# The output products of a second MoE with both halves of each weight side by side as 512 moving columns

## The chip, the cores and the metric

The kernel runs on one core of one Trainium2 chip. The metric is the device time of one launch in microseconds (us), from the host's order to the end of the last store. Before the change it is 1485.99 us, the median of three runs (1485.76 to 1487.83).

Engines are named as in the profile: PE (TensorE: matmuls, and PEld its weight loads), DVE (VectorE), ACT (ScalarE), POOL, and SP (SyncE), whose queue here issues every DMA of the kernel. In a matmul the stationary operand ("weights" to PE) is loaded first, 128x128; the other operand moves through the array column by column, up to 512 columns, and the product is added up in a PSUM bank of 2 KB per partition, of which there are eight.

## The reference

An attention block writes 4352 tokens of 512 numbers (8 groups of 512 tokens and 32 states). They go through a first MoE (512 to 2048, squared ReLU, back to 512) and then a second one, whose back half is what is changed here:

```
xn  = x / sqrt(mean(x*x) + 1e-6) * rms_g
g   = xn @ w_gate          # 512 -> 1536
val = xn @ w_val
out = (g / (1 + exp(-g)) * val) @ w_out     # 1536 -> 512
```

## The kernel before

All matrix products keep nearly the precision of fp32: each operand is split in a high part `hi` (a cast, on ACT) and a low part `lo` (the rest, a subtraction on DVE; `split`, lines 121 to 123), and each product is three matmuls, hi·hi, hi·lo and lo·hi. The second MoE also multiplies 2x2 block matrices with seven products in place of eight (`PRODUCTS`): sums of the blocks are made before (`wq_sums`, `w2_sums`, `h_sums`), and `recombine` (lines 580 to 600) adds the seven products up after.

The second MoE's front half (`moe2_in`, line 718) runs over four pairs `s` of token groups, and twelve chunks `fc` of 128 of the 1536 hidden numbers, with line 126 to 128 matmuls of 512 moving columns. Its results are stored in DRAM as `hq_dr[s, m]`, six chunks `m` of seven 128x512 blocks each (four blocks of the matrix and three of their sums; `h_store`, lines 780 and 781). The 32-token states of all groups together are a block of 256 tokens, which stays in SBUF (`hs`).

The back half begins with that state block (`moe2_out_sb`): 72 matmuls of 512 columns with the plain weights, of which it needs tiles 0 and 1 of each `m` alone. Then come eight blocks of 256 tokens of each group of a pair (`moe2_out`). For each block and each `m` two loads bring the seven blocks back (`hb`, four of them, 512 KB, line 834; `hc`, three, 384 KB, line 835), ACT and DVE split them, and for each of the seven products `k` and each half `c` of 128 tokens three matmuls of 256 columns follow (line 859): the token block is stationary, the weights move. The seven products of a block fill seven PSUM banks for all six `m`; at the last `m` `recombine` empties them in `ox` and `oy`, which are stored with 512 KB each (line 877).

The weights of the back half, `w2`, are summed and split while the first MoE runs, kept in DRAM, and loaded into SBUF near the end of the front half (line 816; four tiles of 512 KB for each `m`: tiles 0 and 1 the hi and lo of the four plain blocks, tiles 2 and 3 the hi and lo of the sums).

What runs in which order is written out: every step is put at a position (`put(pos, step)`), in units of one step of the matmul loop, all are sorted, and each engine gets its instructions in that order. The offsets stand in the table `T` (`wq` is the load of the front half's weights, `hst` the stores of `hq_dr`, `w2l` the weights' loads, `hbl` and `hbs` the loads and the splits of the back half). SP's queue is strictly in that order as well: a store that waits for DVE holds up all the loads behind it. `u(...)` takes one of 54 slots of 4 KB per partition in SBUF.

Of the kernel before, what the change touches and what calls it, by code (L numbers as in the profile page):

```python
# [57 lines left out]
def attention_moe_kernel(  # L58
# [521 lines left out]
    def hi_of(t, n=None):  # L580
        hi = u([P, 2, 512], F32R, "hi")
        src = f(t) if n is None else f(t)[:, :n, :]
        nc.scalar.copy(hi if n is None else hi[:, :n, :], src)
        return hi

    def lo_of(t, hi):
        lo = u([P, 2, 512], F32R, "lo")
        nc.vector.tensor_tensor(lo, f(t), f(hi), op=ALU.subtract)
        return lo
# [147 lines left out]
            hg[s, fc] = y  # L737

    def moe2_in_sb(fc):
        cols = slice((fc % 2) * P, (fc % 2 + 1) * P)  # L740
# [12 lines left out]
        product(v, "s1", "b11", True)  # L753
        product(v, "a22", "t4", False)
        q, r = divmod(fc, 4)
        if r == 0:
            hs[q] = u([P, 4, 256], F32, "hs")
        t = u([P, 2, 512], F32, "rg")
        nc.scalar.activation(t[:, 0, :n], g, AF.Silu)
        nc.vector.tensor_tensor(hs[q][:, r, :], t[:, 0, :n], v, op=ALU.mult)  # L760

    def h_sums(s, m):

# [11 lines left out]
    def h_store(s, m):  # L775
# [28 lines left out]

    def w2_split(m, i):
        after(("w2s", m, i))
        t = w2s[m][i]
        hi = hi_of(t)
        lo = lo_of(t, hi)
        nc.sync.dma_start(w2_dr[m, 2 * i], f(hi))  # L810
        nc.sync.dma_start(w2_dr[m, 2 * i + 1], f(lo))

    def load_w2(m, i):
        after(("ldw2", m, i), ("w2s", m, i // 2))
        w2q[m, i] = u([P, 2, 512], F32R, "w2")
        nc.sync.dma_start(f(w2q[m, i]), w2_dr[m, i])  # L816

    B_AT = dict(b11=(0, 0), b21=(0, 2), b22=(0, 3), t1=(2, 0), t2=(2, 1), t3=(2, 2), t4=(2, 3))

    def w2_part(m, name):  # L820
        i, q = B_AT[name]
        return tuple(
            w2q[m, i + j].rearrange("p a (q m) -> p (a q) m", q=2)[:, q, :] for j in range(2)
        )


    hb = {}

    def load_hb(blk, m):
        s, ob = divmod(blk, 2)  # L830
        cols = slice(256 * ob, 256 * ob + 256)
        after(("ldhb", blk, m), ("hst", s, m))
# [3 lines left out]
        hb[blk, m] = t  # L836

    def split_hb(blk, m, i):
        t = hb[blk, m][i]
        n = 4 - i  # L840
        hi, lo = u([P, 4, 256], F32R, "hh"), u([P, 4, 256], F32R, "hl")
        split(t[:, :n, :], hi[:, :n, :], lo[:, :n, :])
        hb[blk, m][i] = (hi, lo)
# [3 lines left out]
    def moe2_out(blk, m, k):
        a, b = PRODUCTS[k]
        last = m == NF2 // 2 - 1
        if m == 0:  # L850
            acc2[blk, k] = any_bank("o2")
        ps = acc2[blk, k]
        i, q = divmod(A_ROW.index(a), 4)
        hi, lo = (t[:, q, :] for t in hb[blk, m][i])
        w_hi, w_lo = w2_part(m, b)
# [9 lines left out]
        if not last:  # L865
# [4 lines left out]
        pv = ps.rearrange("p (c d) -> p c d", c=2)  # L870
        recombine(k, pv, (ox[:, :, :256], ox[:, :, 256:]), (oy[:, :, :256], oy[:, :, 256:]))
        s, ob = divmod(blk, 2)
        for i, done in ((0, 5), (1, 6)):
            if k == done:
                b = 2 * s + i
                rows = out[b * NT : b * NT + S, :].rearrange("(p c) m -> p c m", c=4)
                nc.sync.dma_start(rows[:, 2 * ob : 2 * ob + 2, :], acc2[blk][i])

    def split_hs(q):
        hi, lo = u([P, 4, 256], F32R, "hh"), u([P, 4, 256], F32R, "hl")  # L880
        split(hs[q], hi, lo)
        hs[q] = (hi, lo)

    def moe2_out_sb(fc):
        if fc == 0:
            acc2[SB, 0], acc2[SB, 1] = any_bank("o2"), any_bank("o2")
        q, r = divmod(fc, 4)
        hi, lo = hs[q]
        w_hi, w_lo = w2q[fc // 2, 0][:, fc % 2, :], w2q[fc // 2, 1][:, fc % 2, :]
        for c in range(2):  # L890
            cols = slice(c * P, (c + 1) * P)
            mm3(acc2[SB, c], hi[:, r, cols], lo[:, r, cols], w_hi, w_lo, fc == 0, fc == NF2 - 1)
        if fc < NF2 - 1:
            return
        t = u([P, 2, 512], F32, "os")
        nc.scalar.copy(t[:, 0, :], acc2[SB, 0])
        nc.vector.tensor_copy(t[:, 1, :], acc2[SB, 1])
        for c in range(2):
            for q in range(4):
                r0 = (4 * c + q) * NT + S  # L900
                nc.sync.dma_start(out[r0 : r0 + NS, :], t[32 * q : 32 * q + 32, c, :])
# [101 lines left out]
    for fc in range(NF2):
        put(n2 + fc / 2, moe2_out_sb, fc)
    for q in range(NF2 // 4):
        put(n2 + 2 * q + T["hs"], split_hs, q)
    for blk in range(B):
        e = n2 + (blk + 1) * nout
        for m in range(nout):
            for k in range(7):  # L1010
                put(e + m + k / 7, moe2_out, blk, m, k)
            put(e + m + T["hbl"], load_hb, blk, m)
            put(e + m + T["hbs0"], split_hb, blk, m, 0)
            put(e + m + T["hbs1"], split_hb, blk, m, 1)
# [168 lines left out]
```

## Time and profile before

| what | value |
|---|---|
| median of three runs | 1485.99 us |
| the profiled execution, its own time | 1484.66 us |
| its span, first to last instruction | 1482.6 us |
| granted TensorE clock, mean | 0.990 |
| PE busy | 1447.2 us, 98% of the span |
| DVE, ACT busy | 76%, 53% |
| the state block of the back half, PE | 1216.4 to 1232.6 us |
| its eight blocks, PE | 1232.6 to 1477 us |

The span is about 2.1 us shorter than the execution's own time. PE's busy time counts a matmul until its modelled end, and these ends overlap the next matmul, so a matmul's cost is read from the distance of two starts in the timeline, not from its length. A row of waits names who ended an idle time; a row of the chain names what the end of the program rests on.

### The profile page before, as it was taken

What the parts mean: (1) busy time and instruction counts of PE and PEld (TensorE: products, weight loads), DVE (VectorE), ACT (ScalarE), POOL (GpSimd) and SP (SyncE); (2) the same over time, 40 slices, a digit from 0 to 9 for tenths busy, and PEclk for the clock granted to TensorE, in tenths of its full rate; (3) what the DMA queues carried; (4) which work ended last, traced back from release to release, by engine and by line L of the source; (5) the groups of instructions that cost most, each with busy time, mean ns of one, the idle gap of its engine ahead of it and who ended that gap; (6) DMA issues with size and microseconds to landing.
All of it is one profiled execution on the core that took longest, in us unless ns stands there. A gap on an engine that the chain in (4) does not pass through costs nothing. (4 is left out here: it accounts for less than half of the span.)

```text
span 1482.6 us, 20652 instructions
## 1 busy us (share of the span) xinstructions
PE 1447.2 (98%) x7706; PEld 1248.6 (84%) x7706; DVE 1125.2 (76%) x1654; ACT 783.0 (53%) x1186; POOL 0.7 (0%) x6
## 2 busy tenths in 40 slices
PE   4899999999999999999999999999999999999998
PEld 2688888888888888889987888888888888999998
DVE  7997878999998999874778878978965664565554
ACT  5988768888888888874522211312311123434331
POOL 0000000000000000000000000000000000000000
PEclk7999999999999999999999999999999999999999
DMA  8886443464555555452957897797786869567753
GB/s 321 291 282 226 149 163 121 163 235 166 226 176 219 178 220 180 170 208 72 355 213 279 324 347 282 284 354 279 264 315 221 292 238 339 182 218 242 241 188 107
DMA packets 138420, 345.82 MB, mean 233 GB/s; under 512 B 12112, under 2 KB 56144, under 8 KB 138320
## 3 DMA queue, kind: packets, MB, share of 16 engines
q1 hardware_dynamic: 138320, 344.51, 64.6%
q8 instruction: 60, 0.98, 0.3%
q14 instruction: 40, 0.33, 0.1%
HBM read 229.12 MB, written 115.34 MB: 232 GB/s over the span
## 5 line engine op out<-in xcount | busy, mean ns | idle before, releaser
L126 PE MATMUL p<-hi,wq 128*128 128x512 f32 x672 | 261.7, 389 | 2.0 <-DVE hx L594 2.0
L127 PE MATMUL p<-lo,wq 128*128 128x512 f32 x672 | 261.6, 389 | 0.0
L128 PE MATMUL p<-hi,wq 128*128 128x512 f32 x672 | 261.4, 389 | 0.0
L859 PE MATMUL o<-w,hh 128*128 128x256 f32 x1344 | 242.1, 283 | 0.8 <-ACT hh L122 0.8
L734 ACT ACTIVATE hx<-hx 128x1024 f32<-128x1024 f32 x48 | 50.9, 1061 | 332.9 <-DVE hx L594 332.9
L126 PE MATMUL o<-hl,wh 128*128 128x512 f32 (+1 forms) x576 | 218.8, 380 | 1.1 <-DVE x L518 0.8
L128 PE MATMUL o<-hl,wl 128*128 128x512 f32 (+1 forms) x576 | 217.6, 378 | 0.0
L127 PE MATMUL o<-hl,wh 128*128 128x512 f32 (+1 forms) x576 | 217.5, 378 | 0.0
L859 PEld LDWEIGHTS o<-w,hh 128*128 128x128 f32 x1344 | 209.6, 192 | 1.3 <-ACT hh L122 1.3
L859 PE MATMUL o<-w,hl 128*128 128x256 f32 x672 | 190.4, 283 | 0.8 <-DVE hl L123 0.8
L594 DVE TENSOR_TENSOR hx<-hx,p 128x512 f32<-128x512 f32 x192 | 128.9, 683 | 52.6 <-PE p L128 49.6
L126 PEld LDWEIGHTS p<-hi,wq 128*128 128x128 f32 x672 | 126.2, 188 | 28.2 <-DVE hx L594 2.4
L128 PEld LDWEIGHTS p<-hi,wq 128*128 128x128 f32 x672 | 126.2, 188 | 26.4
L127 PEld LDWEIGHTS p<-lo,wq 128*128 128x128 f32 x672 | 126.2, 188 | 25.5
L490 DVE TENSOR_TENSOR hl<-rg,hl 128x512 fp32r<-128x512 f32 (+1 forms) x144 | 94.6, 657 | 54.3 <-ACT hl L489 53.4
L859 PEld LDWEIGHTS o<-w,hl 128*128 128x128 f32 x672 | 129.0, 192 | 1.1 <-DVE hl L123 1.0
L126 PEld LDWEIGHTS o<-hl,wh 128*128 128x128 f32 x576 | 108.4, 188 | 22.8 <-DVE x L518 2.8
L128 PEld LDWEIGHTS o<-hl,wl 128*128 128x128 f32 x576 | 108.4, 188 | 20.3
L127 PEld LDWEIGHTS o<-hl,wh 128*128 128x128 f32 x576 | 108.4, 188 | 19.8
L126 PE MATMUL h<-at,ph 128*128 128x512 f32 x256 | 102.1, 399 | 5.0 <-ACT pst L260 5.0
L123 DVE TENSOR_TENSOR hl<-hb,hh 128x1024 fp32r<-128x1024 f32 x48 | 58.7, 1222 | 57.1 <-ACT hh L122 57.1
L122 ACT CAST hh<-hb 128x1024 fp32r<-128x1024 f32 x48 | 50.4, 1050 | 95.9 <-DMA hb<-hq_dr 94.6
(169 smaller groups left out, 2592.9 us busy)
## 6 DMA issues: line engine op xcount, KB each, us to landing
wq<-wq_dr SPq DMA_DIRECT2D x168, 512.0 KB, 7.2
hq_dr<-hy SPq DMA_DIRECT2D x48, 512.0 KB, 3.6
hb<-hq_dr SPq DMA_DIRECT2D x48, 512.0 KB, 8.5
hc<-hq_dr SPq DMA_DIRECT2D x48, 384.0 KB, 8.7
raw<-in_moe_w_out_dram SPq DMA_DIRECT2D x30, 512.0 KB, 6.6
p_dr<-pst SPq DMA_DIRECT2D x56, 256.0 KB, 5.5
praw<-p_dr SPq DMA_DIRECT2D x28, 512.0 KB, 5.3
wq_dr<-hi SPq DMA_DIRECT2D x24, 512.0 KB, 2.9
```

The costliest lines, as they stand in the source:

```text
L122: nc.scalar.copy(hi, src)
L123: nc.vector.tensor_tensor(lo, src, f(hi), op=ALU.subtract)
L126: nc.tensor.matmul(ps, lh, rh, start=start, stop=False)
L127: nc.tensor.matmul(ps, lh, rl, start=False, stop=False)
L128: nc.tensor.matmul(ps, ll, rh, start=False, stop=stop)
L490: nc.vector.tensor_tensor(t[:, 1, :n], rg[:, 1, :n], f(t[:, 0, :n]), op=ALU.subtract)
L594: add = lambda o, i, p: nc.vector.tensor_tensor(o, i, p, op=ALU.add)
L734: nc.scalar.activation(x, x, AF.Silu)
L859: mm = lambda l, r, start, stop: nc.tensor.matmul(o, l, r, start=start, stop=stop, skip_group_check=True)
```

## The change

The changed kernel keeps the number of products, and each product's three terms, but feeds PE in other pieces. The hi and the lo of a block of `w2` now lie side by side in 512 columns (`w2_split` writes them so, `load_w2` brings three full tiles and one half tile for each `m`). A product of 128 tokens is then one matmul of 512 columns (the tokens' hi against hi and lo of the weights) and one of 256 (the tokens' lo against the weights' hi, into the first half of the bank). The two halves of the bank are added at the very end, on DVE, in `os` (line 893), which is stored with 256 KB.

A bank now holds 128 tokens, not 256, so there are 17 blocks, the states as the first of them: they go through the seven products too, with `hs_sums` (four DVE operations of 128x128 for each `m`), and need all the tiles of `w2`. Within a block the six `m` are done in two halves of three, product by product. Loads are for a pair of blocks (256 tokens, as before), splits for each block of 128 (128x512 and 128x384). Several offsets of `T` differ.

```
-    wq0=-6.06, wq=-1.9, wq_gap=0.27,
+    wq0=-6.06, wq=-4.0, wq_gap=0.33,
...
+    def hs_sums(m):
...
+        nc.vector.tensor_tensor(a[4], a[1], a[3], op=ALU.add)
+        sub(5, 4, 0)
+        sub(1, 0, 1)
+        sub(6, 2, 5)
...
     def load_w2(m, i):
-        after(("ldw2", m, i), ("w2s", m, i // 2))
-        w2q[m, i] = u([P, 2, 512], F32R, "w2")
-        nc.sync.dma_start(f(w2q[m, i]), w2_dr[m, i])
-    B_AT = dict(b11=(0, 0), b21=(0, 2), b22=(0, 3), t1=(2, 0), t2=(2, 1), t3=(2, 2), t4=(2, 3))
+        after(("ldw2", m, i), ("w2s", m, i))
+        n = 1 if i == 3 else 2
+        w2q[m, i] = u([P, 2, 2, 256], F32R, "w2")
+        nc.sync.dma_start(f(w2q[m, i])[:, :n], w2_dr[m, i][:, :n])
+    B_AT = dict(b11=(0, 0), b21=(0, 1), t1=(1, 0), t2=(1, 1), t3=(2, 0), t4=(2, 1), b22=(3, 0))
...
-        for c in range(2):
-            o = ps[:, 256 * c : 256 * c + 256]
-            cols = slice(c * P, (c + 1) * P)
-            mm = lambda l, r, start, stop: nc.tensor.matmul(
+        for m in range(half * HALF, (half + 1) * HALF):
+            hi, lo = hq[blk, m]
+            w = w2_part(m, b)
+            mm = lambda o, l, r, start, stop: nc.tensor.matmul(
                 o, l, r, start=start, stop=stop, skip_group_check=True
             )
-            mm(hi[:, cols], w_hi, m == 0 and c == 0, False)
-            mm(hi[:, cols], w_lo, False, False)
-            mm(lo[:, cols], w_hi, False, last)
+            mm(ps, hi[:, i, :], w, m == 0, False)
+            mm(ps[:, :256], lo[:, i, :], w[:, :256], False, m == 2 * HALF - 1)
...
+                o = u([P, 2, 256], F32, "os")
+                nc.vector.tensor_tensor(o, t[:, :, :256], t[:, :, 256:], op=ALU.add)
...
+    for q, blk in enumerate([2 * B] + list(range(2 * B))):
+        e = n2 + q * nout
         for m in range(nout):
+            h, r = divmod(m, HALF)
+            if blk < 2 * B and blk % 2 == 0:
+                put(e + HALF * h + T["hbl"] + T["hbl_gap"] * r, load_hb, blk // 2, m)
+            put(e + HALF * h + T["hbs"] + T["hbs_gap"] * r, split_hb, blk, m)
```

How the order moves is shown at three places. In the rows a name carries the tile's numbers (`w2_dr5_3` is `m` 5, tile 3; `hq_dr0_1` pair 0, `m` 1; numbers behind a second underscore only count tiles), and an L is the line in the kernel concerned.

The first place is SP's queue at the passage from the front half to the back half. Before, behind the four stores of `hq_dr3_4`:

```order
L816 DMA w2_2150_11112<-w2_dr5_1_192 128x1024
L816 DMA w2_2153_11120<-w2_dr4_2_189 128x1024
L816 DMA w2_2154_11122<-w2_dr3_3_186 128x1024
L780 DMA hq_dr3_5_170<-hy_2116_10901 128x1024
L780 DMA hq_dr3_5_170<-hy_2133_11003 128x1024
L780 DMA hq_dr3_5_170<-sa_2151_11114 128x1024
L781 DMA hq_dr3_5_170<-sa_2152_11115 128x512
L816 DMA w2_2157_11150<-w2_dr5_2_193 128x1024
L816 DMA w2_2158_11152<-w2_dr4_3_190 128x1024
L834 DMA hb_2159_11160<-hq_dr0_0_147 128x4x256
L835 DMA hc_2160_11161<-hq_dr0_0_147 128x3x256
L816 DMA w2_2161_11170<-w2_dr5_3_194 128x1024
```

After, behind the same four stores and two full loads (`w2_dr4_2` and `w2_dr5_0`):

```order
L830 DMA w2_2163_11191<-w2_dr4_3_190 128x512
L830 DMA w2_2164_11193<-w2_dr5_1_192 128x1024
L830 DMA w2_2171_11217<-w2_dr5_2_193 128x1024
L849 DMA hb_2173_11226<-hq_dr0_0_147 128x4x256
L850 DMA hc_2174_11227<-hq_dr0_0_147 128x3x256
L793 DMA hq_dr3_5_170<-hy_2123_10953 128x1024
L793 DMA hq_dr3_5_170<-hy_2142_11062 128x1024
L793 DMA hq_dr3_5_170<-sa_2159_11181 128x1024
L794 DMA hq_dr3_5_170<-sa_2160_11182 128x512
L849 DMA hb_2175_11234<-hq_dr0_1_148 128x4x256
L850 DMA hc_2176_11235<-hq_dr0_1_148 128x3x256
L830 DMA w2_2177_11238<-w2_dr5_3_194 128x512
```

The last tile of the weights, `w2_dr5_3`, stands behind one more pair of `hb` and `hc` loads than before, and the state block now needs it; the loads of the first blocks, `hb` and `hc` of `hq_dr0_0`, moved ahead of the stores of `hq_dr3_5`.

The second place is a turn from one 256 tokens to the next. SP's queue before, with the stores of the first block of pair 0:

```order
L877 DMA out_0_dram<-ox_2216_11534 128x1024
L877 DMA out_0_dram<-oy_2217_11535 128x1024
L834 DMA hb_2225_11601<-hq_dr0_4_151 128x4x256
L835 DMA hc_2226_11602<-hq_dr0_4_151 128x3x256
L834 DMA hb_2237_11661<-hq_dr0_5_152 128x4x256
L835 DMA hc_2238_11662<-hq_dr0_5_152 128x3x256
L834 DMA hb_2243_11715<-hq_dr1_0_153 128x4x256
L835 DMA hc_2244_11716<-hq_dr1_0_153 128x3x256
L834 DMA hb_2249_11769<-hq_dr1_1_154 128x4x256
L835 DMA hc_2250_11770<-hq_dr1_1_154 128x3x256
L834 DMA hb_2255_11823<-hq_dr1_2_155 128x4x256
L835 DMA hc_2256_11824<-hq_dr1_2_155 128x3x256
```

After, from the stores of a block that is the first of its two:

```order
L903 DMA out_0_dram<-os_2335_12102 128x512
L903 DMA out_0_dram<-os_2336_12112 128x512
L849 DMA hb_2348_12168<-hq_dr1_0_153 128x4x256
L850 DMA hc_2349_12169<-hq_dr1_0_153 128x3x256
L849 DMA hb_2350_12172<-hq_dr1_1_154 128x4x256
L850 DMA hc_2351_12173<-hq_dr1_1_154 128x3x256
L849 DMA hb_2352_12176<-hq_dr1_2_155 128x4x256
L850 DMA hc_2353_12177<-hq_dr1_2_155 128x3x256
L849 DMA hb_2364_12250<-hq_dr1_3_156 128x4x256
L850 DMA hc_2365_12251<-hq_dr1_3_156 128x3x256
```

Before, the stores of a block are followed by loads for `m` 4 and 5 of the next block and for the first of the one after it. After, the stores of the first block of 128 tokens are followed by the loads of the next 256 tokens from `m` 0 on; all six `m` are behind these stores, and the next two stores are behind all of them.

DVE's order around these stores after the change, with the sums of the first block of two (`ox`, `oy`, `os`) and the splits for the second (`hl`):

```order
L595 TENSOR_TENSOR oy_2328_12046<-ox_2327_12045,o2_2318_11992 128x512
L124 TENSOR_TENSOR hl_2332_12069<-hb_2292_11862,hh_2331_12068 128x512
L124 TENSOR_TENSOR hl_2332_12069<-hc_2293_11863,hh_2331_12068 128x384
L595 TENSOR_TENSOR ox_2327_12045<-ox_2327_12045,o2_2321_12005 128x512
L595 TENSOR_TENSOR oy_2328_12046<-oy_2328_12046,o2_2321_12005 128x512
L124 TENSOR_TENSOR hl_2334_12083<-hb_2294_11866,hh_2333_12082 128x512
L124 TENSOR_TENSOR hl_2334_12083<-hc_2295_11867,hh_2333_12082 128x384
L595 TENSOR_TENSOR ox_2327_12045<-ox_2327_12045,o2_2324_12018 128x512
L595 TENSOR_TENSOR ox_2327_12045<-ox_2327_12045,o2_2325_12025 128x512
L893 TENSOR_TENSOR os_2335_12102<-ox_2327_12045 128x512
L595 TENSOR_TENSOR oy_2328_12046<-oy_2328_12046,o2_2326_12032 128x512
L893 TENSOR_TENSOR os_2336_12112<-oy_2328_12046 128x512
```

The stores of the two `os` stand at the end of the sums of a block, behind the splits of the next block's first three `m`.

The third place is SP's queue in the first pair of the front half. Before:

```order
L657 DMA wq_1480_7615<-wq_dr4_2_135 128x1024
L657 DMA wq_1484_7636<-wq_dr4_3_136 128x1024
L780 DMA hq_dr0_2_149<-hy_1435_7369 128x1024
L780 DMA hq_dr0_2_149<-hy_1450_7446 128x1024
L780 DMA hq_dr0_2_149<-sa_1467_7547 128x1024
L781 DMA hq_dr0_2_149<-sa_1468_7548 128x512
L657 DMA wq_1487_7660<-wq_dr4_6_139 128x1024
L657 DMA wq_1494_7685<-wq_dr5_0_140 128x1024
```

After:

```order
L658 DMA wq_1470_7559<-wq_dr4_6_139 128x1024
L658 DMA wq_1474_7571<-wq_dr5_0_140 128x1024
L560 DMA xn_dr8_102<-x2_1388_7139 128x2x256
L658 DMA wq_1477_7592<-wq_dr5_1_141 128x1024
L658 DMA wq_1482_7617<-wq_dr5_4_144 128x1024
L658 DMA wq_1485_7637<-wq_dr5_5_145 128x1024
L560 DMA xn_dr8_102<-x2_1387_7136 128x2x256
L658 DMA wq_1491_7668<-wq_dr5_2_142 128x1024
L658 DMA wq_1494_7687<-wq_dr5_3_143 128x1024
L793 DMA hq_dr0_2_149<-hy_1442_7407 128x1024
L793 DMA hq_dr0_2_149<-hy_1457_7484 128x1024
L793 DMA hq_dr0_2_149<-sa_1479_7603 128x1024
```

The load of `wq_dr4_6` stood behind the four stores of `hq_dr0_2`. After the change it stands nine rows ahead of the first of them, and six loads of `wq_dr5` stand ahead of them too.

## Rows read from the trace of the kernel before

**Rows 1.** Busy time of each engine over the span, the page's first part.

```profile
PE 1447.2 (98%) x7706; PEld 1248.6 (84%) x7706; DVE 1125.2 (76%) x1654; ACT 783.0 (53%) x1186; POOL 0.7 (0%) x6
```

**Rows 2.** Waits of PE from 600 us to the end: total, times, longest.

```profile
PE p L126 <- DVE hx L594: 2.0, 1, 2.0
PE o L859 <- ACT hh L122: 0.8, 1, 0.8
PE o L859 <- DVE hl L123: 0.8, 1, 0.8
```

**Rows 3.** Windows of the back half: busy (count) by engine, PEclk, DMA share, GB/s.

```profile
1216.40:1232.60 16.20, 16.20 (x74) 13.32 (x72) 5.19 (x7) 1.12 (x2) 0.00 (x0) 1.00 1.04 401
1232.60:1477.00 244.40, 242.81 (x2018) 242.08 (x2016) 133.79 (x152) 91.23 (x105) 0.00 (x0) 1.00 0.65 211
```

**Rows 4.** Chain that ended last: start us, us, what.

```profile
1224.56 7.99 DMA hb<-hq_dr
...
1234.99 241.38 PE o L859 x2008
```

**Rows 5.** Timeline of PE in the front half: start us, us, line, operation.

```profile
1040.17 0.39 PE L126 MATMUL p<-hi,wq 128*128 128x512 f32 x1
1040.40 0.39 PE L127 MATMUL p<-lo,wq 128*128 128x512 f32 x1
```

**Rows 6.** Timeline of PE at 807 us.

```profile
807.49 0.47 PE L126 MATMUL p<-hi,wq 128*128 128x512 f32 x1 [1.99 <-DVE hx L594]
```

**Rows 7.** One load of wq, by its tile: issue, time to landing.

```profile
L657 SPq DMA_DIRECT2D wq<-wq_dr x1: 392/392/392, 797.9 to 797.9; - x1
...
DMA to landing us min/median/max: 9.4/9.4/9.4
```

**Rows 8.** Last load of w2, by its tile.

```profile
L816 SPq DMA_DIRECT2D w<-w_dr x1: 467/467/467, 1225.8 to 1225.8; - x1
...
DMA to landing us min/median/max: 9.2/9.2/9.2
```

**Rows 9.** Windows at the passage and at a turn, columns as in rows 3.

```profile
1228.40:1234.40 6.00, 5.00 (x22) 3.68 (x20) 0.69 (x1) 1.68 (x2) 0.00 (x0) 1.00 1.05 365
...
1430.00:1434.00 4.00, 4.00 (x36) 4.00 (x35) 3.39 (x4) 2.73 (x4) 0.00 (x0) 1.00 1.09 350
```

**Rows 10.** Windows around an idle time of PE, columns as in rows 3.

```profile
36.50:40.70 4.20, 0.02 (x1) 0.00 (x0) 4.00 (x8) 4.16 (x8) 0.00 (x0) 0.81 1.03 412
40.70:45.90 5.20, 5.20 (x12) 4.13 (x13) 5.01 (x9) 5.17 (x10) 0.00 (x0) 0.50 0.13 50
...
805.50:807.50 2.00, 0.01 (x1) 0.04 (x1) 2.00 (x5) 0.00 (x0) 0.00 (x0) 1.00 1.03 422
```

**Rows 11.** Timeline of DVE in the back half.

```profile
1447.26 0.68 DVE L594 TENSOR_TENSOR ox<-ox,o 128x512 f32<-128x512 f32 x1
1447.86 0.95 DVE L123 TENSOR_TENSOR hl<-hc,hh 128x768 fp32r<-128x768 f32 x1
1448.73 0.68 DVE L594 TENSOR_TENSOR ox<-ox,o 128x512 f32<-128x512 f32 x1
```

**Rows 12.** Timeline of SP at a turn.

```profile
1389.31 0.35 SPq L877 DMA_DIRECT2D out_dram<-ox  x1
...
1390.35 0.62 SPq L834 DMA_DIRECT2D hb<-hq_dr  x1
```

**Rows 13.** Timeline of ACT at the same turn.

```profile
1396.64 1.05 ACT L122 CAST hh<-hb 128x1024 fp32r<-128x1024 f32 x1 [8.94 <-DMA hb<-hq_dr]
...
1399.27 1.05 ACT L122 CAST hh<-hb 128x1024 fp32r<-128x1024 f32 x1 [0.69 <-DMA hb<-hq_dr]
```

**Rows 14.** All hb loads: time to landing.

```profile
DMA to landing us min/median/max: 4.0/8.5/11.2
```

**Rows 15.** Timeline of the end, PE and SP.

```profile
1476.79 0.28 PE L859 MATMUL o<-w,hl 128*128 128x256 f32 x1
...
1478.27 0.35 SPq L877 DMA_DIRECT2D out_dram<-oy  x1
```

More of the change, by code (lines that the diff above doesn't have):

```diff
@@ L739, in moe2_in_sb @@
     def moe2_in_sb(fc):
+        after(("sb", fc))
         cols = slice((fc % 2) * P, (fc % 2 + 1) * P)
@@ L754, in moe2_in_sb @@
         product(v, "a22", "t4", False)
-        q, r = divmod(fc, 4)
+        m, r = divmod(fc, 2)
         if r == 0:
-            hs[q] = u([P, 4, 256], F32, "hs")
+            hs[m] = u([P, 7, P], F32, "hs")
         t = u([P, 2, 512], F32, "rg")
         nc.scalar.activation(t[:, 0, :n], g, AF.Silu)
-        nc.vector.tensor_tensor(hs[q][:, r, :], t[:, 0, :n], v, op=ALU.mult)
+        both = hs[m][:, 2 * r : 2 * r + 2, :]
+        halves = lambda ap: ap.rearrange("p (c t) -> p c t", c=2)
+        nc.vector.tensor_tensor(both, halves(t[:, 0, :n]), halves(v), op=ALU.mult)
+    def hs_sums(m):
+        after(("hs", m), ("sb", 2 * m), ("sb", 2 * m + 1))
+        a = [hs[m][:, i, :] for i in range(7)]
+        sub = lambda o, i, j: nc.vector.tensor_tensor(a[o], a[i], a[j], op=ALU.subtract)
+        nc.vector.tensor_tensor(a[4], a[1], a[3], op=ALU.add)
+        sub(5, 4, 0)
+        sub(1, 0, 1)
+        sub(6, 2, 5)
     def h_sums(s, m):
@@ L784, in attention_moe_kernel @@
     w2_dr = {
-        (m, i): dram.tile([P, 2, 512], F32, tag=f"w2_{m}_{i}", name=f"w2_dr{m}_{i}")
+        (m, i): dram.tile([P, 2, 2, 256], F32, tag=f"w2_{m}_{i}", name=f"w2_dr{m}_{i}")
         for m in range(NF2 // 2)
@@ L835, in load_hb, with split_hb, moe2_out @@
         nc.sync.dma_start(t[1][:, :3, :], hq_dr[s, m][:, 4:, cols])
[L836 to L843, printed above, removed]
+        hb[g, m] = t
+    def split_hb(blk, m):
+        hi, lo = u([P, 7, P], F32R, "hh"), u([P, 7, P], F32R, "hl")
+        if blk == 2 * B:
+            after(("hsplit", m), ("hs", m))
+            split(hs.pop(m), hi, lo)
+        else:
+            g, c = divmod(blk, 2)
+            t = hb[g, m]
+            cols = slice(c * P, (c + 1) * P)
+            split(t[0][:, :, cols], hi[:, :4, :], lo[:, :4, :])
+            split(t[1][:, :3, cols], hi[:, 4:, :], lo[:, 4:, :])
+        hq[blk, m] = (hi, lo)
     acc2 = {}
[L847 removed]
+    HALF = NF2 // 4
+    def moe2_out(blk, half, k):
         a, b = PRODUCTS[k]
[L849 to L850 removed]
+        if half == 0:
             acc2[blk, k] = any_bank("o2")
         ps = acc2[blk, k]
[L853 to L859 removed]
+        i = A_ROW.index(a)
+        for m in range(half * HALF, (half + 1) * HALF):
+            hi, lo = hq[blk, m]
+            w = w2_part(m, b)
+            mm = lambda o, l, r, start, stop: nc.tensor.matmul(
                 o, l, r, start=start, stop=stop, skip_group_check=True
             )
[L862 to L865 removed]
+            mm(ps, hi[:, i, :], w, m == 0, False)
+            mm(ps[:, :256], lo[:, i, :], w[:, :256], False, m == 2 * HALF - 1)
+        if half == 0:
             return
@@ L869, in moe2_out @@
         ox, oy = acc2[blk]
-        pv = ps.rearrange("p (c d) -> p c d", c=2)
-        recombine(k, pv, (ox[:, :, :256], ox[:, :, 256:]), (oy[:, :, :256], oy[:, :, 256:]))
-        s, ob = divmod(blk, 2)
+        recombine(k, ps, (ox[:, 0, :], ox[:, 1, :]), (oy[:, 0, :], oy[:, 1, :]))
         for i, done in ((0, 5), (1, 6)):
             if k == done:
[L875 to L901, printed above, removed]
+                t = acc2[blk][i]
+                o = u([P, 2, 256], F32, "os")
+                nc.vector.tensor_tensor(o, t[:, :, :256], t[:, :, 256:], op=ALU.add)
+                flat = o.rearrange("p a d -> p (a d)")
+                if blk == 2 * B:
+                    for q in range(4):
+                        r0 = (4 * i + q) * NT + S
+                        nc.sync.dma_start(out[r0 : r0 + NS, :], flat[32 * q : 32 * q + 32, :])
+                    continue
+                s, c = divmod(blk, 4)
+                r0 = (2 * s + i) * NT
+                rows = out[r0 : r0 + S, :].rearrange("(p c) m -> p c m", c=4)
+                nc.sync.dma_start(rows[:, c, :], flat)
     sources = {"win": w_in, "wout": w_out, "wg": w_gate, "wv": w_val, "w2": w_out2}
@@ L1002, in attention_moe_kernel @@
     nout = NF2 // 2
[L1003 to L1008, printed above, removed]
-        for m in range(nout):
+    for m in range(nout):
+        put(n2 - NF2 + 2 * m + 2 + T["hss"], hs_sums, m)
+    for q, blk in enumerate([2 * B] + list(range(2 * B))):
+        e = n2 + q * nout
+        for m in range(nout):
+            h, r = divmod(m, HALF)
+            if blk < 2 * B and blk % 2 == 0:
+                put(e + HALF * h + T["hbl"] + T["hbl_gap"] * r, load_hb, blk // 2, m)
+            put(e + HALF * h + T["hbs"] + T["hbs_gap"] * r, split_hb, blk, m)
+        for h in range(2):
             for k in range(7):
[L1011 to L1014, printed above, removed]
+                put(e + HALF * (h + k / 7), moe2_out, blk, h, k)
     for m in range(nout):
@@ L1061, in attention_moe_kernel @@
         put(pos + T["e_sum"], w2_sums, c2)
-        for i in range(2):
+        for i in range(4):
             put(pos + T["e_sp"] + T["e_spgap"] * i, w2_split, c2, i)
```

30 lines of the change are left out of this document (15 added, 15 removed).

## The prediction

> **What bounds the kernel now.** I read the page's first part first: PE is busy 1447.2 us, 98% of the span [rows 1]. Then the waits of PE from 600 us on: three in all, of 2.0, 0.8 and 0.8 us [rows 2]. Then the back half by windows: 16.2 us of the state block and 244.4 us of the eight blocks, PE busy in nearly all of it, DVE in 133.8 us (55%), at the full granted clock [rows 3]. The chain of waits ends with 241.38 us of nothing but line 859 on PE, 2008 matmuls, and ahead of these stands one `hb` load of 7.99 us [rows 4]. So a matmul saved there is time saved, as long as loads and DVE keep out of the chain. Loads are what to watch: the one of [rows 4] landed 16.2 us after the state block had begun (1216.4 to 1232.55).
>
> **The matmuls.** A matmul of 512 columns starts 0.2267 us (between 0.22 and 0.23) after the one before it [rows 5]; one of 256 takes 241.38 / 2008 = 0.1202 [rows 4]. At 2.4 GHz the columns are 0.2133 and 0.1067, so each matmul has some 13.4 ns besides, whatever its length. Before: 72 × 0.2267 + 2016 × 0.1202 = 16.3 + 242.3 = 258.6 us. After: 17 blocks × 6 × 7 = 714 pairs of (0.2267 + 0.1202) = 247.7 us. That is **−10.9 us**: 660 fewer matmuls (8.9) and 4608 fewer columns (1.9). A block of 128 tokens takes 42 × 0.347 = 14.57 us, a half of it 7.28, one product of a half 1.04.
>
> The Trainium skill (TensorE: Matmul & The Clock Gate, section "Wait — 56ns, not 53.3ns?") gives a warm matmul columns / 2.4 GHz plus about 2.5 ns, 215.7 ns at 512; the trace has 226.7 there [rows 5]. By the page's fixed part the 660 would be worth an estimated 1.7 us and the term −3.6; the measured row decides.
>
> **The wait at 807 us.** PE stands 2.0 us there, put down to a DVE sum [rows 2, 6]. But one load of `wq` that stood on SP behind the stores of `hq_dr0_2` was issued at 797.9 and landed 9.4 us later, at 807.3 [rows 7], just ahead of PE's restart. After, that load is nine rows ahead of the stores. I take the load as the cause: **−2.0 us** (0 if it was the sum).
>
> **The passage to the back half.** The state block needed tiles 0 and 1 of `w2` alone; now it needs all of them, the last (`w2_dr5_3`) for the sixth product at the last `m`: 7.28 + 5 × 1.04 + 2 × 0.347 = 13.2 us after its start. When does it land? DMA is full all through here, share 1.04 [rows 3]. In units of 512 KB, before had behind the stores of `hq_dr3_4`: three loads, 3.5 units of stores, two loads and `hb`, 9.5 units, done 16.2 us after the state block's start. After has 2 + 0.5 + 2 loads, `hb` and `hc` (1.75), 3.5 of stores, 1.75 again, and 0.5: 12.0 units. The 2.5 more take 1.31 us each at the 401 GB/s of [rows 3] or 1.44 at the 365 of [rows 9]: landing at +19.5 to +19.8. (Before's own last `w2` load landed 9.2 us after 1225.8, at +18.6 [rows 8], and nobody waited for it.) PE thus stands about 6.4 us. Then it has 1.4 us left of the state block, and the first block's `m` 0 to 2 follow; `m` 2 stands behind the late tile with 1.75 units of its own (2.6 us at the pace below), then a cast and a subtraction: about 1.6 us more, and some 0.6 at `m` 5. Total about 8.6, where before lost 1.6 [rows 2]: **+7.0 us**. Bounds: if the stores of `hq_dr3_5` do not hold the queue and DMA runs at its best, 5 us in all (+3.4). A stall of this length can also cost clock: after PE stood 4.2 us early in the kernel, twelve matmuls took 5.20 us at a granted clock of 0.50, 2.5 us more than twelve at 0.2267; after a stand of 2.0 us the clock was 1.00 [rows 10]. With that on top, 10.5 (+9). The part of it that falls in the 2.2 us of waiting behind the stall is hidden, so I stay at +7.0.
>
> **The turns from 256 tokens to the next.** Before, SP issues loads about a block ahead. After, all six loads of the next 256 tokens stand behind the stores of the first of two blocks, and these wait for DVE. From PE's end of that block, step by step:
> DVE's backlog. From the first sum of a block up to the second `os` it has nine operations of 128x512 and three pairs of splits (512 elements take 0.60 to the next start, 768 take 0.87 [rows 11], 384 on the same line 0.47). That is 5.4 + 3.2 = 8.6, and some 0.4 between dependent ones, begun 2.3 us into PE's last half of 7.28 (the second product's end and a little): 4.0 us late.
> Issue: two stores and the `hb` load behind them take 1.04 us before, from 1389.31 to 1390.35 [rows 12]; the first store no longer counts, being issued earlier: 0.45.
> First landing: its cast began 6.3 us after the issue [rows 12, 13], behind 1 MB of stores; now it is half of that, 1.3 us less at 401 GB/s: 4.95 (least of all such loads 4.0 [rows 14], most 6.3).
> Five more `m`: the casts follow 2.63 us apart [rows 13] (917 KB at the 350 GB/s of [rows 9]): 13.15.
> Cast and subtraction of `m` 5: 0.6 and 0.7 (half of the 1.05 of [rows 13] and a little; 0.68 [rows 11]): 1.3.
> Sum 23.85 us. PE needs `m` 5 after the second block and a half, with two pairs and its first matmul: 14.57 + 7.28 + 0.69 + 0.23 = 22.8. It stands 1.1 us, at each of seven turns: **+7.7 us**. Bounds: with the first landing at 4.0 or DVE less late, 0; with 6.3, 2.4 each, +17. `m` 2 would be 0.5 late in the first half already (15.95 against 15.5), which is part of the 1.1.
>
> **What costs nothing.** DVE gets two `os` operations and the sums for 128 instead of 256 tokens: nine of 0.60 and six pairs of 1.07, 11.8 us in 14.57 (81%, 55% before). ACT has six pairs and one copy, half of its time. PE hides both, as seven banks become free product by product through the second half; if that cover went, DVE would set a block's time only above 14.57. `hs_sums` and the splits of the states run while PE is in the front half. The end: last matmul, sum, then `os` (+0.8) and a store of half the size (two of 512 KB now, the last issued at 1478.27, 1.5 us behind the last matmul [rows 15]; 512 KB less in all, 1.3 at 401 GB/s): **−0.5**.
>
> **Sum.** −10.9 − 2.0 + 7.0 + 7.7 − 0.5 = +1.3 us on the profiled execution's 1484.66, thus 1486.0. The median of the runs is 1.33 above that execution, so the forecast is 1487.3 us. What can be told from no change is 0.2%, 3 us: 1483.0 to 1489.0.
>
> **Rivals.**
> *The loads arrive in time.* If DVE is less late than four us or the first load lands at 4.0, the turns cost nothing, since the chain is only 1.1 us behind PE's need: 1487.3 − 7.7 = 1479.6; with a passage of +5 also, 1477.6. For it: DMA's mean share in the eight blocks is 0.65 [rows 3], so the queue has room. Against it: ACT's `hb` casts wait for loads now [rows 13], though a block ahead. About 1479; 24 in 100.
> *Slower: the chain of stores and loads sets the turns.* Behind the stores of the first block every turn takes 4.0 + 0.45 + 6.3 + 13.15 + 1.3 = 25.2 us against 22.8, if the first load is as late as at [rows 12, 13] though the stores are smaller. Then seven turns cost 16.8, +9.1 on the forecast: 1496.4. It decides from 1.5 us per turn on. For it: landings of `hb` reach 11.2 us [rows 14]. Against: those stand in full queues. 18 in 100.
> *DVE becomes the bound.* At 81% it would need its operations 24% slower for that; then each of 16 blocks gains a wait, 1 us each: 1503. None of [rows 11] shows such a time: 3 in 100.
> *The change doesn't give the fixed part.* If the 13.4 ns belong to the weight load (0.19 us of PEld for each, PEld busy 242.1 of 244.4 us [rows 3]), and a 256-column matmul behind a 512-column one waits for it, only 1.9 of the 10.9 is left: 1496.3. Against it, the front half has the same 13.4 ns where PEld is less busy (13.3 of 16.2 in the state block [rows 3]): 3 in 100.
>
> **How the numbers follow.** 52 in 100 for the forecast's own case, with a range of 1483 to 1492 (passage +4 to +9, turns 0.6 to 1.6 us each). Of these 5 fall below 1483.0, 31 within the bound, 16 above 1489.0. The first rival adds 22 faster and 2 within, the other three 24 slower. So faster 0.27, same 0.33, slower 0.40. The range of 8 in 10 goes from 1478 (half of the first rival left out) to 1497 (the tails of the slower ones).
>
> **What would show it.** The profile after should have 7040 matmuls in all but a few missing ones; 512- and 256-column matmuls alternating in the back half with starts 0.347 us apart per pair; no wait near 807 us; one wait of PE of about 6 us some 13 us into the state block, put down to a DMA of `w2`, perhaps with a granted clock of 0.5 behind it; seven waits of about 1 us, 29 us apart, in the second half of every other block, on the splits of `m` 5; DVE about 80% busy. The forecast is wrong if the long wait is missing (then faster by some 6 us), if the turns have no waits, or if the pair of matmuls takes other than 0.347 us.

## The result and the profile after

The changed kernel is slower: 1495.56 us, median of four runs (1494.59 to 1496.10), against 1485.88 for the kernel before on the same chip. The ratio is 1.0063, with a 95% interval of 1.0046 to 1.0080. The time lies in the predicted range (1478 to 1497), near its upper end, and 8.3 us above the forecast.

The profiled execution has a span of 1493.9 us, 11.3 more than [rows 1] belongs to. Waits of PE from 600 us on, as in [rows 2]:

```profile
PE o L878 <- DMA w<-w_dr: 7.5, 1, 7.5
PE o L878 <- ACT hh L123: 3.7, 6, 1.0
PE o L878 <- DVE hl L124: 2.9, 13, 0.2
```

The wait of 2.0 us in the front half is gone; 7.5 us at the weights are new, and nineteen short ones behind them. These name 6.6 us, which is about half of what the turns cost: a named wait is counted only from the modelled end of the matmul before it. So the distance of matmul starts has to be read as well.

The chain of waits through the back half, against [rows 4]:

```profile
1214.95 11.48 PE o L878 x65
1226.43 9.41 DMA w<-w_dr
...
1235.89 33.07 PE o L878 x171
1268.97 8.39 DMA hb<-hq_dr
1277.45 0.63 ACT hh L123
1278.11 0.70 DVE hl L124
...
1278.85 21.08 PE o L878 x118
```

Before it was PE alone for 241 us. Now it goes to a load of the weights once and then, at every turn, to an `hb` load (`m` 5), its cast, its subtraction, and back to PE.

Windows, columns as in [rows 3] (us; busy of PE, PEld, DVE, ACT, POOL; PEclk, DMA share, GB/s):

```profile
1247.58:1269.84 22.26, 22.26 (x129) 19.29 (x127) 16.46 (x29) 9.26 (x19) 0.00 (x0) 1.00 0.48 155
1349.02:1363.58 14.56, 14.56 (x87) 12.84 (x86) 11.01 (x20) 2.99 (x6) 0.00 (x0) 1.00 0.70 223
...
1228.40:1235.90 7.50, 0.01 (x1) 0.01 (x1) 2.03 (x4) 1.51 (x3) 0.00 (x0) 0.73 1.06 381
1235.90:1242.00 6.10, 6.10 (x19) 5.24 (x20) 5.18 (x9) 2.26 (x4) 0.00 (x0) 0.50 1.10 348
1250.00:1480.00 230.00, 223.32 (x1240) 189.18 (x1239) 184.19 (x313) 99.79 (x193) 0.00 (x0) 1.00 0.63 203
```

From the back half's first matmul (1214.79) to its last (1488.80) are 274.0 us; before, 260.4 (1216.39 to 1476.79). 714 pairs at 0.3467 would be 247.5. The other 26.5 are, within rounding: 7.7 of waiting at the passage and 2.9 of slow clock behind it, 12.9 at the seven turns (0.8, 2.4, 1.9, 1.5, 2.1, 2.4, 1.8), and 3.1 because a pair often took longer. Of the 12.9, 7.4 stand in the first half of a block, at the operands of `m` 2, and 5.5 in the second half, at those of `m` 5. The first row holds 63 pairs without a wait in 22.26 us, 0.3533 each; the second 42 in 14.56, 0.3467 each. The numbers in brackets also count matmuls that only reach into a window; the pairs are counted from the starts.

| from the profiles | before | after | difference |
|---|---|---|---|
| up to the state block's first matmul | 1216.4 | 1214.8 | −1.6 |
| from there to the last matmul's start | 260.4 | 274.0 | +13.6 |
| from there to the span's end | 5.8 | 5.1 | −0.7 |

### The profile page after: what moved, and what is told of

It reads as the page before. It is cut to its first block, busy times and chain, and to the rows that moved or that the text cites. A ratio compares the mean times of both kernels' runs of the same rounds, so it can differ in the third digit from the quotient of the medians.

```text
span 1493.9 us, 19689 instructions
## 1 busy us (share of the span) xinstructions
PE 1448.3 (97%) x7046; PEld 1213.2 (81%) x7046; DVE 1200.2 (80%) x1885; ACT 799.7 (54%) x1305; POOL 0.7 (0%) x6
## 4 chain that ended last, share of the span: by engine, by line
PE 75%; DVE 10%; DMA 6%; ACT 6%; issue 1%; SPq 1%; ACTq 0%; DVEq 0%
PE o L878 13%; PE p L128 10%; PE p L127 10%; PE p L129 10%; PE o L127 5%; PE o L129 5%; PE o L128 5%; DMA hb<-hq_dr 4%; PE h L127 3%; PE h L128 3%; PE h L129 3%; DVE hl L491 1%; DVE pl L124 1%; ACT rg L488 1%; PE pps L128 1%
## 5 line engine op out<-in xcount | busy, mean ns | idle before, releaser
L878 PE MATMUL o<-w,hh 128*128 128x512 f32 x714 | 255.7, 401 | 11.3 <-DMA w<-w_dr 7.5
L878 PE MATMUL o<-w,hl 128*128 128x256 f32 x714 | 202.8, 284 | 2.9 <-DVE hl L124 2.9
L878 PEld LDWEIGHTS o<-w,hh 128*128 128x128 f32 x714 | 135.4, 190 | 46.2 <-DMA w<-w_dr 7.8
L878 PEld LDWEIGHTS o<-w,hl 128*128 128x128 f32 x714 | 136.2, 191 | 7.3 <-DVE hl L124 7.3
L128 PEld LDWEIGHTS o<-hl,wh 128*128 128x128 f32 x576 | 108.4, 188 | 19.8
L127 PE MATMUL h<-at,ph 128*128 128x512 f32 x256 | 102.1, 399 | 5.4 <-ACT pst L261 5.3
L128 PE MATMUL h<-at,ph 128*128 128x512 f32 x256 | 100.4, 392 | 0.0
L129 PE MATMUL h<-at,pl 128*128 128x512 f32 x256 | 100.3, 392 | 0.0
```

The source lines that it names most:

```text
L127: nc.tensor.matmul(ps, lh, rh, start=start, stop=False)
L128: nc.tensor.matmul(ps, lh, rl, start=False, stop=False)
L129: nc.tensor.matmul(ps, ll, rh, start=False, stop=stop)
L878: mm = lambda o, l, r, start, stop: nc.tensor.matmul(o, l, r, start=start, stop=stop, skip_group_check=True)
```

## The experiments

**Are the turns caused by the loads' place behind the stores?** Theory A says yes, and that the stores wait for DVE; rival B says that the DMA's pace or DVE's load sets them, whatever the order. In the changed kernel the third turn reads so, in one timeline (start us, us, engine and line, what):

```profile
1320.76 0.69 DVE L893 TENSOR_TENSOR os<-oy 128x512 f32<-128x512 f32 x1
...
1321.92 0.38 SPq L849 DMA_DIRECT2D hb<-hq_dr  x1
...
1326.71 0.62 ACT L123 CAST hh<-hb 128x512 fp32r<-128x512 f32 x1
...
1330.64 0.62 ACT L123 CAST hh<-hb 128x512 fp32r<-128x512 f32 x1 [1.05 <-DMA hb<-hq_dr]
...
1333.28 0.62 ACT L123 CAST hh<-hb 128x512 fp32r<-128x512 f32 x1 [1.04 <-DMA hb<-hq_dr]
1333.95 0.49 PE L878 MATMUL o<-w,hh 128*128 128x512 f32 x1 [0.69 <-ACT hh L123]
1334.68 0.39 PE L878 MATMUL o<-w,hl 128*128 128x256 f32 x1 [0.24 <-DVE hl L124]
...
1341.14 0.62 ACT L123 CAST hh<-hb 128x512 fp32r<-128x512 f32 x1 [1.00 <-DMA hb<-hq_dr]
...
1342.54 0.39 PE L878 MATMUL o<-w,hl 128*128 128x256 f32 x1 [0.18 <-DVE hl L124]
```

The block of PE ended at 1317.55. DVE's second `os` ends at 1321.45, 3.9 us later; the first `hb` is issued at 1321.92; its cast stands at +4.8 us; the next one comes 3.9 us behind it, then they follow some 2.6 apart; PE stands 1.5 us at `m` 2 (1333.95 and 1334.68); `m` 5 is cast at 1341.14, and PE stands 0.45 us more ahead of 1342.54. Two experiments, the first with the loads in another place:

```
-                put(e + HALF * h + T["hbl"] + T["hbl_gap"] * r, load_hb, blk // 2, m)
+                hbl = T["hbl"] if blk == 0 else -7.5
+                put(e + HALF * h + hbl + T["hbl_gap"] * r, load_hb, blk // 2, m)
```

> The loads of the next 256 tokens (m 0 to 2, then m 3 to 5) are put right behind the splits that free their buffers, m 0 to 2 ahead of the two stores of the first block. Theory A (the turns wait because the loads stand behind these stores, which wait for DVE's sums, and six loads at 2.6 us each then take longer than PE's block and a half): m 0 is issued some 8 us earlier, so the waits at the seven turns, 12.9 us in the changed kernel (1.84 per turn), fall to 3 us or less, and the time from 1495.6 to about 1484. Rival B (the turns are bound by the pace of the DMA or by DVE's 80% whatever the order of the queue): the waits stay above 9 us and the time above 1492.

Measured 1482.13 us (ratio to the kernel before 0.9969, 0.9956 to 0.9981). The window from the second block on:

```profile
1247.60:1470.00 222.40, 222.40 (x1261) 192.96 (x1260) 181.82 (x316) 95.11 (x196) 0.00 (x0) 1.00 0.64 210
```

PE is busy in all of its 222.4 us, and no distance of two starts shows a wait: no turn waits any more. By the medians 13.4 us are gained, but the ten runs go from 1477.03 to 1484.53, and what spreads them is not shown. The profiled one, 1484.53, is 11.2 under the changed kernel's profiled one: the 12.9 of the turns, less 1.6 because every pair took 0.3533 in it; its passage costs 10.6, as before the edit. B falls: the same loads at the same pace and DVE's load (182 of 222 us) are hidden.

The second shortens DVE's part of the chain, by leaving the last addition out:

```
-                o = u([P, 2, 256], F32, "os")
-                nc.vector.tensor_tensor(o, t[:, :, :256], t[:, :, 256:], op=ALU.add)
+                flat = t[:, :, :256]
...
```

> The final addition of the two halves of a bank (os, line 893) is left out, and the first half stored, so the hi by lo terms are missing from the output. Theory A: DVE's sums end 1.2 to 1.5 us earlier behind a block, and so do the stores and the loads behind them; each turn's wait falls from 1.84 to about 0.5 us, 8 to 9 us in all, time about 1487. Rival B (DMA pace alone): the waits at the turns stay within 2 us of 12.9 and the time above 1493. The waits at the passage do not change in either.

Measured 1485.12 us, 10.4 less than the changed kernel. Its waits from the second block on:

```profile
PE o L878 <- DVE hl L124: 1.1, 5, 0.2
PE o L878 <- ACT hh L123: 0.6, 2, 0.3
```

1.7 us are left of the 6.6 named above; by the matmuls' starts the turns cost 5.2 in place of 12.9, 7.7 less where 8 to 9 were expected. So some 1.3 us less of DVE's work in each block was worth 1.1 us at each turn, as A has it; of the rest of the 10.4, 1.3 is that the pairs went at 0.3467 in more of this run.

**What makes the passage long?** Theory A: a full queue of DMA, so that what goes ahead makes something else late; rival C: the one late tile of the weights. First that tile alone was moved ahead:

```
-            put(n2 + T["w2l"] + T["w2l_gap"] * m + T["w2l_i"] * i, load_w2, m, i)
+            at = T["w2l"] + T["w2l_gap"] * m + T["w2l_i"] * i
+            put(n2 + min(at, 1.8), load_w2, m, i)
```

> Only the last tile of the weights, w2_dr5_3, is put ahead of the first hb loads and of the stores of hq_dr3_5. Theory A (the passage is a full DMA queue; what is moved ahead makes other loads late): the wait of 7.5 us at the weights goes, but PE then waits for the hb and hc of m 1 and m 2 of the first block, which land as late as before; gain 1 to 4 us, time 1492 to 1495. Rival C (the one tile was the cost): the wait of 7.5 us and the 2.9 us of slow clock behind it go, time about 1485.

Measured 1495.34 us, no change. Waits of PE there, and the window behind the longer of them:

```profile
PE o L878 <- ACT hh L123: 7.0, 2, 5.3
```

```profile
1234.60:1241.90 7.30, 5.55 (x14) 3.84 (x15) 6.15 (x11) 2.77 (x5) 0.00 (x0) 0.50 1.10 349
```

The wait at the weights is gone and 7.0 us at the casts of `m` 1 and `m` 2 have come, with the clock at 0.50 again. By the starts the passage costs 10.4 us in place of 10.6; the turns cost 14.3 in place of 12.9, with a slow clock at the third. C falls. A holds, and even its 1 to 4 us of gain did not come.

Then the stores that nobody needs soon were taken out of the way as well, on top of both edits above:

```
-                put(e + fc + 1 + T["hst"], h_store, s, fc // 2)
+                late = 4 if s == B // 2 - 1 and fc == NF2 - 1 else 0
+                put(e + fc + 1 + T["hst"] + late, h_store, s, fc // 2)
```

> The loads ahead of the stores as in the first experiment, the last weight tile ahead of the first hb loads, and the stores of hq_dr3_5, which nobody needs soon, behind all loads of the first 256 tokens. Theory A (the passage is DMA queue: 3.5 units of 512 KB less ahead of m 1 and m 2, 4.6 to 5 us): no wait at the weights, one of about 4 to 5 us at m 1 and m 2 of the first block in place of 8.4, perhaps still with a slow clock behind it; time 1482.1 less 4 to 6, about 1477. Rival (the order within the full queue does not matter, or the stores' buffers held up bring new waits): within 2 us of 1482.

Measured 1478.62 us (0.9944, 0.9929 to 0.9959), 3.5 less than with the turns alone repaired; 4 to 6 were expected. Four runs (1477.13 to 1478.96) stand here against the ten that spread so widely, and their ranges overlap; the two profiles tell it better. By the starts the passage costs 6.0 us in place of 10.6, so 4.6 less. Windows at the passage:

```profile
1228.00:1232.40 4.40, 2.35 (x12) 1.41 (x10) 3.51 (x6) 1.83 (x4) 0.00 (x0) 0.95 1.10 348
1232.40:1239.00 6.60, 6.60 (x20) 5.29 (x21) 6.18 (x12) 2.78 (x5) 0.00 (x0) 0.52 1.10 351
1239.00:1245.00 6.00, 6.00 (x37) 5.26 (x36) 2.01 (x4) 2.62 (x6) 0.00 (x0) 1.00 0.79 297
```

PE now loses 2.7 us in waits, but still 3.2 to a clock of about 0.5 for 6.6 us. The queue's part is as A has it. That the stores alone, without the tile ahead, would do it was not tried.

Last, on top of that, the first block was given another order of work, to take up `hb` at the pace at which it lands:

```
+        step = 1 if blk == 0 else HALF
+        for h in range(0, nout, step):
             for k in range(7):
-                put(e + HALF * (h + k / 7), moe2_out, blk, h, k)
+                put(e + h + step * k / 7, moe2_out, blk, range(h, h + step), k)
```

> As the one before, and the first block of 128 tokens goes m by m (seven products for each) instead of three m at a time, so that it takes up hb at 2.4 us for each m, about the pace at which the loads land (2.6). Theory A: PE waits only for m 0 and little for the others, 1 to 2 us in all, time about 1473 to 1474; the clock does not fall. Rival: the first block waits for the last m anyway (its loads are late as a whole): the wait only moves to m 3 to 5, time as in passage_reordered.

Measured 1479.65 us: no gain. The two long waits have other names (timeline of PE):

```profile
1232.40 0.47 PE L878 MATMUL o<-w,hh 128*128 128x512 f32 x1 [2.72 <-DVE oy L595]
...
1234.34 0.80 PE L878 MATMUL o<-w,hh 128*128 128x512 f32 x1 [1.35 <-DVE ox L595]
```

Neither theory had this: all seven products of `m` 0 want a PSUM bank within 2.5 us, and the banks are still held by the state block, whose sums DVE does between the splits. The wait turned from a DMA's into a bank's.

**Was it the load of `wq` that PE waited for at 807 us?** In the kernel before, one number was changed (`wq=-1.9` to `wq=-2.2`), which puts that load ahead of the four stores.

> The kernel before with one number changed (wq -1.9 to -2.2): the load of wq_dr4_6 in the first pair comes ahead of the four stores of hq_dr0_2, as in the changed kernel. Theory L (PE's 2.0 us at 807 us are the wait for this load): the wait is gone or under 0.3 us, the span some 1.6 to 2.0 us shorter, time about 1484. Rival (it was DVE's sums): the wait of 2 us stays where it was.

Measured 1483.67 us (0.9985, 0.9975 to 0.9996). Waits of PE from 600 us on:

```profile
PE o L859 <- ACT hh L122: 0.9, 1, 0.9
PE o L859 <- DVE hl L123: 0.8, 1, 0.8
PE h L127 <- DVE at L123: 0.2, 1, 0.2
```

The 2.0 us are gone and 2.3 of time. The number moves the other loads of `wq` by 0.3 of a step too, but none of DVE's sums: it was the load.

**What is a pair of matmuls worth?** Theory P: 0.3533 in place of 0.3467 comes from the alternation of lengths; Q: it is a state taken up at a wait and kept. In one run the matmuls were grouped by length (three of 512, then three of 256):

```
             mm(ps, hi[:, i, :], w, m == 0, False)
+        for m in range(half * HALF, (half + 1) * HALF):
+            lo, w = hq[blk, m][1], w2_part(m, b)
             mm(ps[:, :256], lo[:, i, :], w[:, :256], False, m == 2 * HALF - 1)
```

> Within a product and a half the three matmuls of 512 columns come first and then the three of 256, in place of alternating; the same work. In the changed kernel a pair of matmuls took 0.3533 us in some stretches and 0.3467 in others, 3.1 us in all over 0.3467. Theory P (the alternation of lengths costs the 6.7 ns): every pair takes 0.3467, 3 us less, 1492.5. Rival Q (the 6.7 ns come from how PE takes up its work after a wait): both paces are there as before, time within 1.5 us of 1495.6. Other bound: each step costs more, as lo operands are now needed later and hi ones earlier; at the turns that gives less than 0.7 us each.

Measured 1494.66 us (1491.94 to 1495.74), not told apart from the changed kernel. Timeline of PE:

```profile
1289.69 0.86 PE L878 MATMUL o<-w,hh 128*128 128x512 f32 x3
1290.38 0.52 PE L878 MATMUL o<-w,hl 128*128 128x256 f32 x3
1290.74 0.86 PE L878 MATMUL o<-w,hh 128*128 128x512 f32 x3
```

Three pairs take 1.05 us, 0.350 each: neither of the two paces, and neither theory's number. A second order, with 256 ahead of 512 at `m` 1 and `m` 4, was tried on the kernel with the turns repaired:

```
-            mm(ps, hi[:, i, :], w, m == 0, False)
-            mm(ps[:, :256], lo[:, i, :], w[:, :256], False, m == 2 * HALF - 1)
+            one = lambda: mm(ps, hi[:, i, :], w, m == 0, False)
+            two = lambda: mm(ps[:, :256], lo[:, i, :], w[:, :256], False, m == 2 * HALF - 1)
+            for step in (two, one) if m in (1, 4) else (one, two):
+                step()
```

> As the first experiment (loads ahead of the stores; there every pair of matmuls took 0.3533 us, 4.7 us in all over 0.3467), but at m 1 and m 4 the matmul of 256 columns comes ahead of that of 512, so lengths change less often. Theory P (the length's change from one matmul to the next costs it): pace 0.350 or less per pair, 2 us or more off 1482. Rival Q (the pace is a state that PE falls into at a wait and keeps): 0.3533 or 0.3467 throughout.

Measured 1480.48 us (1479.26 to 1482.91), 1.65 less by the medians than without it, which the wide range of those runs does not tell from nothing; but the trace has 0.3512 a pair from 1260 us on: P's direction, but not its 0.350. Why the pace is what it is stays open. What it is worth could be measured. On the reordered kernel the matmul of 512 was taken apart again:

```
-            mm(ps, hi[:, i, :], w, m == 0, False)
+            mm(ps[:, :256], hi[:, i, :], w[:, :256], m == 0, False)
+            mm(ps[:, 256:], hi[:, i, :], w[:, 256:], False, False)
```

> The reordered kernel (passage_reordered, 1478.6 us) with the matmul of 512 columns taken apart into two of 256, as before the change: three of 256 for each product and m, same bank, same order. The prediction's theory (each matmul has 13.4 ns besides its columns, so 714 more cost 714 x 13.4 ns): 9.5 us slower, 1488. Theory of the slow pace (a pair takes 0.3533 us, three of 256 take 0.3606): 714 x 0.0073 = 5.2 us slower, about 1484. The clock at the passage may fall in either.

Measured 1482.54 us, 3.9 more than the 1478.62 with 512 columns. The timeline of PE shows three of 256 in 0.36 us, as before:

```profile
1300.02 0.40 PE L878 MATMUL o<-w,hh 128*128 128x256 f32 x2
1300.26 0.28 PE L878 MATMUL o<-w,hl 128*128 128x256 f32 x1
1300.38 0.40 PE L878 MATMUL o<-w,hh 128*128 128x256 f32 x2
```

Over the whole back half three of 256 took 0.3600 us and a pair in passage_reordered 0.3531. So laying hi and lo side by side saves 0.0069 us for each product and `m` at the pace of this kernel, not 0.0134: 4.9 us in all. The run shows 3.9, because waits and slow clock at its passage cost 4.8 us in place of 6.0. This falls to the theory of the slow pace (5.2 expected), and rules out the prediction's 9.5.

Last came the reordered kernel with the serpentine order:

> The reordered kernel with the serpentine order of the matmuls (256 ahead of 512 at m 1 and m 4). There a pair took 0.3512 us in place of 0.3533. If that pace holds: 714 x 0.0021 = 1.5 us less than 1478.6, about 1477. Rival: the order of a first block's matmuls asks for lo earlier and adds waits at the passage, 1478 to 1480.

Measured 1477.16 us (0.9941 of the kernel before, 0.9925 to 0.9957): faster than both kernels, 8.9 us under the one before and 18.4 under the changed one. The serpentine order's own part, 1.5 us by the medians, is not clear of the spread of four runs each (1476.33 to 1478.92 against 1477.13 to 1478.96). Every part of the change is in it; only the order of loads, stores and matmuls differs.

## Why the prediction was right or wrong

The forecast was 1487.3 us, a change too small to tell; slower had 40 chances in 100, the same 33, faster 27. The time came out on the slower side, 8.3 us above the forecast: the passage and the turns were named and cost more than taken, and the matmuls saved less. The slower rival's 1496.4 is within a microsecond of the measured time, but by luck: its turns were to cost 16.8 us, and 12.9 of them came, the rest is slow clock and the pace of a pair. On the profiled execution, +9.8 us over the sum of 1486.0:

- *The matmuls*, −10.9: the step "each matmul has some 13.4 ns besides, whatever its length" failed. It holds for rows of one length ([rows 4, 5], and again with three of 256), not for 512 and 256 in turn. The pair was 0.3467 or 0.3533; 3.1 us of the term were missing here, and where nearly every pair took 0.3533, 4.6 of the 9.5 (three_of_256 against passage_reordered). By its own sign ("if the pair of matmuls takes other than 0.347 us") the forecast was wrong here. The rival in which the fixed part isn't given came in part true; whether by the weight load it named is not shown. By the fixed part of about 2.5 ns that the Trainium skill gives (TensorE: Matmul & The Clock Gate, section "Wait — 56ns, not 53.3ns?") the saving would have been smaller still; no row here has a part so small.
- *The wait at 807 us*, −2.0: right, shown by before_wq_ahead (−1.6 in the profile, 2.3 in the runs).
- *The passage*, +7.0: right in mechanism, 8.3 in size (10.6 against some 2.3 before, by the starts). The last tile landed 21.1 us after the state block's start (1226.43 + 9.41 against 1214.79), not 19.5 to 19.8. The last of the four stores from which the units were counted was issued so, first before, then after:

```profile
1209.13 1.10 SPq L781 DMA_DIRECT2D hq_dr<-sa  x1
...
1211.81 1.31 SPq L794 DMA_DIRECT2D hq_dr<-sa  x1
```

  Its issue ended 6.2 us ahead of the state block before and 1.7 after; the working took this distance as unchanged. From there 9.5 units took 22.3 us and 12.0 took 22.7. So of the 4.9 us by which the landing moved, 4.5 are the later stores; why the 2.5 units more added only 0.4 is not shown, and that the sum came near the landing is in good part luck. The change sets `hst` from 1.47 to 1.88; with some 9.5 us for a step there (two steps lie between the stores of `hq_dr3_3` and these, 1190.50 to 1209.58), the place alone would be an estimated 3.9 us, but this was not tried. The clock fell to 0.50 for 6.1 us, and the waits that were to hide this did not come; that PE at half speed gave the loads time to catch up is likely, but was not tried.
- *The turns*, +7.7: right in mechanism, 12.9 in size, shown by loads_before_stores and no_final_add. At the turn shown DVE's lateness (3.9 for 4.0), the issue (0.47 for 0.45) and the first cast (4.8 for 4.95) came as worked out. The step that failed is "five more `m`: the casts follow 2.63 us apart": that is the pace of a stream in full run. The first interval was 3.9, 1.3 more; the chain took 25.0 us from the end of PE's block to PE's late start where 23.85 were worked out, while PE, at 0.3533 a pair, came to its need some 0.4 later than 22.8. The other turns differ in where the time goes: the first cast stood at 4.7 to 5.6 us (at 5.5 or more in the last three, where the first interval was 2.6), and that of `m` 5 at 18.1 to 19.8, in the mean 18.9, where 4.95 + 13.15 = 18.1 were worked out. At some 0.7 more per turn, most of it from there, this is the 5.2 us that were missing. Of its waits at the turns PE spent more at `m` 2 (7.4 us) than at `m` 5 (5.5); the forecast had expected all of its seven waits at `m` 5 but 0.5 us each. In the windows, columns as before, the DMA comes up only over the first five microseconds, and so it does at all seven turns (127 to 190 GB/s in the first 2.6 us, 266 to 328 in the next):

```profile
1321.90:1324.50 2.60, 2.60 (x17) 2.23 (x16) 2.60 (x6) 0.00 (x0) 0.00 (x0) 1.00 0.63 175
1324.50:1327.10 2.60, 2.60 (x17) 2.27 (x16) 0.17 (x1) 0.87 (x2) 0.00 (x0) 1.00 1.00 298
1327.10:1329.70 2.60, 2.60 (x17) 2.28 (x16) 1.36 (x3) 0.74 (x2) 0.00 (x0) 1.00 1.06 355
```

- *The slower rival* had the place and the mechanism (stores ahead of loads at each turn) and its point, 1.5 us per turn; the turns were at 1.84. Its reason was wrong: the first load's cast stood at 4.7 to 5.6 us, not at 6.3; the stream behind it came up late.
- *DVE as the bound* did not come: 184 us busy of 230, 80% as forecast (81%), and loads_before_stores ran at that share without a wait.
- *The end*, −0.5: −0.7.

The last matmul and the stores behind it, against [rows 15]:

```profile
1488.80 0.28 PE L878 MATMUL o<-w,hl 128*128 128x256 f32 x1
...
1489.49 1.66 SPq L903 DMA_DIRECT2D out_dram<-os  x2
```

The likeliest case was thus chosen on a margin of 1.1 us per turn in a chain of 24, worked out with a pace that only holds once the stream runs.

## What to carry to other kernels

When a block gets smaller and its loads stay as large, look at what stands ahead of these loads in their queue: here two stores, waiting for the last sums of a busy engine, cost 13 us at the turns, which went when six loads were put elsewhere in the order. A saving per instruction that was read where all instructions are of one length must be measured again on the mix that will run. And where DMA was full for 20 us, moving one late tile ahead was worth nothing here; taking transfers out of the queue that nobody needed yet was. When a change also moves offsets, look at where each one puts the transfers that a sum is counted from.

## What the runs showed of the hardware

A pair of 512 and 256 columns starts every 0.3467 or 0.3533 us in the same kernel, for whole stretches, and in the changed kernel's trace goes from one to the other only where PE has waited; uniform rows of 512 (0.2267) and 256 (0.1202) show nothing of the kind. Other orders of the same matmuls gave 0.350 and 0.3512.

The granted clock fell to 1.2 GHz not only behind 7.5 us of waiting, but also in passage_reordered, where PE had been busy for 2.35 us of 4.40 and its longest stand was 1.8 us by the starts (1.5 named); it then stood at about half for 6.6 us. In last_tile_ahead it fell at a turn too (0.58 from 1333.9 to 1338.0), after PE had been busy for 1.09 us of 2.80:

```profile
1331.10:1333.90 2.80, 1.09 (x3) 0.37 (x2) 2.53 (x5) 1.23 (x3) 0.00 (x0) 1.00 1.08 349
```

In the kernel before, a stand of 2.0 us and two of 0.8 us at the passage left it at 1.00 [rows 9, 10].
